# Fewer and larger loads at the start and end of a one-token attention kernel: first K whole, last V in 2 pieces, output projection in 4

## The chip, the cores and the metric

The kernel runs on one core of a Trainium2 chip. The metric is the device time of one execution in microseconds (us). The kernel before took 652.0 us, the median of 3 runs (651.78 to 652.06).

Two numbers are used below. The *time* is the metric. The *span* runs from the first to the last instruction of the trace, and it is listed for every run. The time is 1.3 to 2.0 us longer than the span, and that difference changes from run to run: two runs of the kernel before with a span of 650.3 took 651.69 and 652.32 us.

## The reference

One token attends to a cache of 16384 keys and values with 32 heads of 128, followed by an output projection. A small gated MLP of the same token is mixed in.

```python
# cut: helpers and random inputs
q = (x @ wq).reshape(1, 1, 32, 128).transpose(0, 2, 1, 3)       # x: 1 x 1 x 512, wq: 512 x 4096
scores = einsum('bhqd,bhkd->bhqk', q, k_cache) * 128 ** -0.5    # k_cache: 1 x 32 x 16384 x 128, bf16
p = softmax(scores)
o = einsum('bhqk,bhkd->bhqd', p, v_cache)
a = o.transpose(0, 2, 1, 3).reshape(1, 1, 4096) @ wo            # wo: 4096 x 512
b = ...                                                         # gated MLP of x, width 1792
return g * a + (1 - g) * b                                      # g = sigmoid(sum(x * gate_w))
```

K and V are 134 MB each. Nearly all of the 279.6 MB that the kernel reads is K and V, and each byte is used once.

## The kernel before

The loads go through three large SBUF buffers in a fixed order: K0, K1, V0, K2, V1, K3, V2 and so on, each a pair of heads in 128 partitions of 64 KB (8.39 MB). The last buffer takes the output projection `wo`, 32 rows of 512 per partition. The first K, the last K, the last V and `wo` are cut into pieces, so that work can begin before the whole has landed. Each piece has its own semaphore.

```python
K_CUTS = (0, 128, 256)
V_CUTS = (0, 160, 224, 256)
WO_CUTS = (0, 16, 24, 28, 30, 31, 32)
WIDE = 24
...
    for n, kind, i in loads:                       # issued in order by SyncE
        wait = [user[n - 3]] if n >= 3 else [w_free] if buf[n % 3] is setup else []
        ...
        if n == 0:
            cuts, sems = K_CUTS, ld_kf
        elif i == NP - 1:
            cuts, sems = (K_CUTS, ld_kh) if kind == "k" else (V_CUTS, ld_vp)
        for a, b, done in zip(cuts[:-1], cuts[1:], sems):
            sp.op(lambda e, ...: e.dma_start(out=buf[n % 3][:, a * Dh:b * Dh], in_=src[:, a * Dh:b * Dh]),
                  wait=wait if a == 0 else (), inc=(done, 16))
    for j, (a, b) in enumerate(zip(WO_CUTS[:-1], WO_CUTS[1:])):
        sp.op(lambda e, ...: e.dma_start(out=wo[:, a * D:b * D], in_=wo_src[:, a * D:b * D]), ...)
```

`user[n - 3]` is the last reader of the buffer. V1, for example, goes into K1's buffer, so SyncE issues V1's load when ACT has done the first exponentials of K1. VectorE multiplies a K by the query in four quarters and waits for K data at the first and third. TensorE sums the products; ACT takes the exponentials. A V takes TensorE eight *tiles* of 8 matmuls. TensorE's program is one sequence: the last tiles of the last V, the chain to `o2` (the attention output, transposed for the projection), then the projection.

The projection has two forms. The wide one takes 8 rows in a round of 8 matmuls of 512 columns, spread over four column groups. ACT must then copy the bank, and one more pair of matmuls (`ones` times `d_sb`, the *sum* below) adds the groups up. The narrow one takes a row in two matmuls of 256 columns, straight into the result.

```python
    def pe_wide(e):
        warm(e, 1)                                 # one matmul on zeros
        with e.Fori(0, WIDE // WG) as t:           # rounds of 8 rows
            for j in range(WG): ...                # matmul into d_ps, column group 32 * (j % 4)
            registers_first(nc, n, lambda: take(e, wo_s))   # waits for the piece of wo
            fill(e, 1)                             # one matmul on zeros
    w_ok = act.op(lambda e: e.copy(out=d_sb[:, :], in_=d_ps), wait=[(pe.sem, pe.n)], mark=True)
    ...
    for j, (a, b) in enumerate(zip(WO_CUTS[:-1], WO_CUTS[1:])):
        for k in range(max(a, WIDE), b):           # narrow rows
            y_ok = add(o2[:, k:k + 1], wo[:, k * D:(k + 1) * D], [(ld_o[j], 16)] if k == a else (), k == H - 1)
        if b == 28:
            add(ones_f[:, 0:1], d_sb[:, :], [w_ok])   # the sum
```

The softmax here doesn't subtract the row's maximum and nothing guards it: scores larger than these inputs give would overflow.

Of the kernel before, what the change touches and what calls it, by code (L numbers as in the profile page):

```python
# [15 lines left out]
NP = H // 2  # L16
# [19 lines left out]
NT = NG // TG  # L36
ZB = F // 4
K_CUTS = (0, 128, 256)
V_CUTS = (0, 160, 224, 256)
WO_CUTS = (0, 16, 24, 28, 30, 31, 32)  # L40
WIDE = 24
inv_sqrt_dh = float(Dh) ** -0.5


# [132 lines left out]
def gated_mix_kernel(nc, A_x, A_k_cache, A_v_cache, A_wq, A_wo, B_x, B_w_in, B_w_sp, B_b_sp,  # L177
                     B_w_out, gate_w, out):
    def sb(name, shape, dt):
        return nc.alloc_sbuf_tensor(name, shape, dt)  # L180
# [6 lines left out]
    d_sb = sb("d_sb", [P, 512], FP32)  # L187
# [51 lines left out]
    sem = nc.alloc_semaphore  # L239
# [3 lines left out]
        sem(n) for n in ("ld_x", "ld_g", "ld_q", "ld_w", "ld_u", "st_out"))  # L243
    ld_k = [sem(f"ld_k{b}") for b in range(2)]
    ld_v = [sem(f"ld_v{b}") for b in range(2)]
    ld_kf = [sem(f"ld_kf{b}") for b in range(len(K_CUTS) - 1)]
    ld_kh = [sem(f"ld_kh{b}") for b in range(len(K_CUTS) - 1)]
    ld_vp = [sem(f"ld_vp{b}") for b in range(len(V_CUTS) - 1)]
    ld_o = [sem(f"ld_o{b}") for b in range(len(WO_CUTS) - 1)]
    k_s, v_s, mul_s, red_s, sum_s, exp_s, sl_s, pv_s, drn_s, zer_s, wo_s = (  # L250
        sem(n) for n in ("k_s", "v_s", "mul_s", "red_s", "sum_s", "exp_s", "sl_s", "pv_s", "drn_s",
                         "zer_s", "wo_s"))

    ones_f = nc.const_aps.tensor(1.0, [P, P], FP32)
# [216 lines left out]
    def warm(e, n, again=False):  # L471
        for j in range(n):
            args = (m_ps[0], ident[:, :], zero[:, :])
            flags = dict(start=True, stop=True, skip_group_check=True)
            if j or again:
                matmul_again(nc, e, *args, **flags)
            else:
                e.matmul(args[0], lhsT=args[1], rhs=args[2], **flags)  # L478
# [152 lines left out]
    for n, kind, i in loads:  # L631
        wait = [user[n - 3]] if n >= 3 else [w_free] if buf[n % 3] is setup else []
        src = (k_src if kind == "k" else v_src)[i]
        cuts, sems = (0, KP), [(ld_k if kind == "k" else ld_v)[i % 2]]
        if n == 0:
            cuts, sems = K_CUTS, ld_kf
        elif i == NP - 1:
            cuts, sems = (K_CUTS, ld_kh) if kind == "k" else (V_CUTS, ld_vp)
        for a, b, done in zip(cuts[:-1], cuts[1:], sems):
            sp.op(lambda e, a=a, b=b, n=n, src=src: e.dma_start(  # L640
                out=buf[n % 3][:, a * Dh:b * Dh], in_=src[:, a * Dh:b * Dh]),
                wait=wait if a == 0 else (), inc=(done, 16))
    wo_src = A_wo.rearrange("(p k) n -> p (k n)", k=H)
    for j, (a, b) in enumerate(zip(WO_CUTS[:-1], WO_CUTS[1:])):
        sp.op(lambda e, a=a, b=b: e.dma_start(out=wo[:, a * D:b * D], in_=wo_src[:, a * D:b * D]),  # L645
              wait=[user[wo_at - 3]] if a == 0 else (), inc=(ld_o[j], 16))

    def hand(e, loaded, to, n):
        e.wait_ge(loaded, 16).then_inc(to, n)
        e.nop().then_inc(loaded, -16)  # L650

    def pool_pairs(e):
        for j in range(len(ld_kf)):
            hand(e, ld_kf[j], k_s, 1)
        with e.Fori(0, NP // 2 - 1):
            hand(e, ld_k[1], k_s, 2)
            hand(e, ld_v[0], v_s, NT)
            hand(e, ld_k[0], k_s, 2)
            hand(e, ld_v[1], v_s, NT)
        for j in range(len(ld_kh)):  # L660
            hand(e, ld_kh[j], k_s, 1)
        hand(e, ld_v[0], v_s, NT)
        for j, (a, b) in enumerate(zip(V_CUTS[:-1], V_CUTS[1:])):
            hand(e, ld_vp[j], v_s, (b - a) * NT // KP)

    pool.raw(pool_pairs)


# [17 lines left out]
    def pool_wo(e):  # L686
        e.wait_ge(*d_zero)
        e.wait_ge(*o2_ok)
        for j, (a, b) in enumerate(zip(WO_CUTS[:-1], WO_CUTS[1:])):
            if a < WIDE:  # L690
                hand(e, ld_o[j], wo_s, (min(b, WIDE) - a) // WG)

    pool.raw(pool_wo)

    def pe_wide(e):
        va, pa = (counter(e, n, 0) for n in ("wa", "oa"))
        warm(e, 1)
        with e.Fori(0, WIDE // WG) as t:
            w8 = wo[:, bass.ds(t * (WG * D), WG * D)]
# [12 lines left out]
    pe.raw(pe_wide)  # L712
    pe.n += WIDE // WG
    w_ok = act.op(lambda e: e.copy(out=d_sb[:, :], in_=d_ps), wait=[(pe.sem, pe.n)], mark=True)


    def add(lhsT, rhs, wait, mark=False):
        for s in range(NC):
            ok = pe.op(lambda e, s=s: e.matmul(  # L719
                a_ps[32 * s:32 * s + 1, 0:DQ], lhsT=lhsT, rhs=rhs[:, s * DQ:(s + 1) * DQ],  # L720
                start=False, stop=False, skip_group_check=True), wait=wait if s == 0 else (),
                mark=mark and s == NC - 1, inc=(half, 1) if mark and s == 0 else None)
        return ok

    for j, (a, b) in enumerate(zip(WO_CUTS[:-1], WO_CUTS[1:])):
        for k in range(max(a, WIDE), b):
            y_ok = add(o2[:, k:k + 1], wo[:, k * D:(k + 1) * D],
                       [(ld_o[j], 16)] if k == a else (), k == H - 1)
        if b == 28:
            add(ones_f[:, 0:1], d_sb[:, :], [w_ok])  # L730
    for q in (dve, act):
        mine = range(NC)[:NC // 2] if q is dve else range(NC)[NC // 2:]
        for s in mine:
# [26 lines left out]
def build(inputs):  # L760
    import numpy as _np
    import concourse.bacc as _bacc
    from concourse import mybir as _mybir

    nc = _bacc.Bacc("TRN2", target_bir_lowering=False, num_devices=1, dynamic_dma_scratch_size=4096)
    arrays, args = {}, []
    for name in _INS:
        a = _np.ascontiguousarray(inputs[name])
        if a.dtype.kind in "iu":
            a = a.astype(_np.int64)  # L770
        arrays[f"in_{name}_dram"] = a
        args.append(nc.dram_tensor(f"in_{name}_dram", a.shape, _mybir.dt.from_np(a.dtype), kind="ExternalInput").ap())
    for i, (shape, dtype) in enumerate(_OUTS):
        dt = _mybir.dt.from_np(_np.dtype(dtype))
        args.append(nc.dram_tensor(f"out_{i}_dram", shape, dt, kind="ExternalOutput").ap())
    gated_mix_kernel(nc, *args)
    return nc, arrays
# [9 lines left out]
```

## Time and profile before

| | before |
|---|---|
| time, median of 3 | 652.0 us |
| span of the profiled run | 650.5 us |
| read from HBM | 279.6 MB |
| V1's load issued / K2 landed | 85.3 / 96.4 us |
| last V's pieces landed | 631.1, 636.0, 638.5 us |
| `o2` ready | 642.7 us |
| last row of `wo` landed | 648.53 us |
| result copies start | 648.91 us |

Landing times are those of the load's sixteenth semaphore update in the trace.

The page of the kernel before: span, TensorE's line, and from the 40 slices the granted TensorE clock, the DMA share (tenths) and GB/s, and the summary of the chain that ended last.

```profile
span 650.5 us, 7753 instructions
...
PE 428.0 (66%) x2462; PEld 45.7 (7%) x1320; DVE 336.0 (52%) x159; ACT 45.8 (7%) x112; POOL 2.1 (0%) x10
...
PEclk9978797969779696987969798686988968798999
DMA  9999999999999999999899999999998999999898
GB/s 387 449 429 451 443 395 451 451 387 451 451 439 399 451 451 415 423 451 451 387 451 451 435 403 451 451 391 447 451 451 387 451 451 431 407 419 484 387 433 342
...
DMA 4%; PE 0%; SPq 0%; issue 0%; DVE 0%; ACT 0%; ACTq 0%
...
```

The DMA engines are busy in every slice. The packet records show no gap from 1.3 to 648.0 us. A whole K or V lands 19.35 us after the one before it, which is 433 GB/s. The clock row shows that TensorE, 66% busy, keeps changing between full clock and less.

The chain that ended last, in order of time: start us, us, what.

```profile
...
619.79 27.37 DMA bufs<-in_A_wo_dram
...
647.20 1.36 PE ps_all L719 x18
...
648.57 0.32 PE ps_all L719 x2
...
648.91 0.41 DVE res L734
```

Six loads of `wo` are issued from 618.9, when their buffer comes free, and the rest of the tail hangs on them: 18 matmuls in 1.36 us while the last pieces land, the last two at the last landing, and the copy of the result.

The load of V1 in the timeline (start us, us, engine, line; SPq is SyncE's instruction stream, from which loads are issued):

```profile
...
85.32 0.33 SPq L640 DMA_DIRECT2D bufs<-in_A_v_cache_dram  x1
...
```

Parts of the tail in the timeline (start us, us, engine, line, what; PEld is TensorE's weight load; in brackets the idle time before):

```profile
...
631.27 0.14 PEld L106 LDWEIGHTS ps_all<-bufs,p_t 128*8 x8 [2.13 <-issue]
...
638.64 0.14 PEld L106 LDWEIGHTS ps_all<-bufs,p_t 128*8 x8 [1.45 <-issue]
...
642.47 0.19 DVE L683 CAST o<-ps_all 128x32 bf16<-128x32 f32 x1 [0.35 <-PE ps_all L680]
643.57 0.13 PEld L106 LDWEIGHTS ps_all<-bufs,o 128*1 x8 [1.11 <-issue]
...
```

The last V's first tile starts at 631.27, 0.15 us after the first piece landed. Its eighth starts at 638.64, 0.15 us after the last piece. `o2` is the CAST at 642.47. The first wide round starts at 643.57, when 16 rows of `wo` have landed (643.39), not when `o2` is ready. So the compute waits for the loads at each step.

Four stretches of the tail by engine (busy us, count of instructions, granted clock, DMA share, GB/s); two are shown:

```profile
...
core 0: us, PE busy (x) PEld busy (x) DVE busy (x) ACT busy (x) POOL busy (x), PEclk, DMA share, GB/s
...
641.30:644.70 3.40, 2.10 (x21) 0.70 (x23) 0.60 (x3) 0.00 (x0) 0.00 (x0) 1.00 0.99 417
644.70:648.10 3.40, 2.34 (x32) 0.68 (x24) 0.00 (x0) 0.58 (x1) 0.00 (x0) 1.00 0.95 359
...
```

In this run the clock (PEclk) was full in both.

### The profile page before, as it was taken

Reading aid. Unit: us, or ns where it says so; the run is one execution under the profiler, and the core shown is the slowest. Engines: PE = TensorE matmul, PEld = TensorE weight load, DVE = VectorE, ACT = ScalarE, POOL = GpSimd, SP = SyncE. Lnnn points to the kernel's source line nnn. Section 1 sums busy time; section 2 is a strip of 40 time slices with the busy share of each in tenths; the row PEclk is TensorE's granted clock in tenths of the full one; section 3 lists DMA queues with packets and bytes.
Section 4 is the critical chain, followed back from the end, with each engine's and each line's share of the span. In section 5 each row is a group of like instructions: output and inputs, shape, how many; then the busy total and the mean of one; then the engine's idle time right before and its main releaser. Section 6 shows DMA issues by size and latency. Waiting matters only on the chain. (4 is left out here: it accounts for less than half of the span.)

```text
span 650.5 us, 7753 instructions
## 1 busy us (share of the span) xinstructions
PE 428.0 (66%) x2462; PEld 45.7 (7%) x1320; DVE 336.0 (52%) x159; ACT 45.8 (7%) x112; POOL 2.1 (0%) x10
## 2 busy tenths in 40 slices
PE   0576866847487574757857476585747757478766
PEld 0000010000101000010000101000010100101012
DVE  3587708356281745618265370835629075465600
ACT  2201010000001000010100001000010100001011
POOL 1000000000000000000000000000000000000000
PEclk9978797969779696987969798686988968798999
DMA  9999999999999999999899999999998999999898
GB/s 387 449 429 451 443 395 451 451 387 451 451 439 399 451 451 415 423 451 451 387 451 451 435 403 451 451 391 447 451 451 387 451 451 431 407 419 484 387 433 342
DMA packets 6491, 279.60 MB, mean 430 GB/s; under 512 B 727, under 2 KB 986, under 8 KB 1370
## 3 DMA queue, kind: packets, MB, share of 16 engines
q1 hardware_dynamic: 6482, 279.58, 99.6%
q8 instruction: 1, 0.02, 0.0%
q10 hardware_dynamic: 8, 0.00, 0.0%
HBM read 279.58 MB, written 0.00 MB: 430 GB/s over the span
## 5 line engine op out<-in xcount | busy, mean ns | idle before, releaser
L579 DVE TENSOR_TENSOR bufs<-bufs,qb x64 | 281.4, 4418 | 168.6 <-DVEq L86 168.6
L91 PE MATMUL ps_all<-bufs,ident 128*128 x960 | 265.0, 432 | 0.0
L496 PE MATMUL ps_all<-bufs,ident 128*128 x64 | 28.4, 444 | 150.8 <-PEq L86 150.8
L106 PE MATMUL ps_all<-bufs,p_t 128*8 x1024 | 79.1, 384 | 30.6 <-PEq L86 19.9
L564 DVE TENSOR_REDUCE s_sb<-ps_all 128x64 f32<-128x512 f32 x64 | 44.0, 688 | 97.4 <-DVEq L86 97.4
L91 PE MATMUL ps_all<-zero,ident 128*8 128x512 bf16 (+1 forms) x147 | 56.4, 384 | 0.0
L592 ACT ACTIVATE p_t<-s_sb 64x256 f32 (+1 forms) x32 | 13.3, 414 | 440.2 <-ACTq L86 439.8
L496 PEld LDWEIGHTS ps_all<-bufs,ident 128*128 128x128 bf16 x64 | 6.3, 99 | 368.0 <-issue 368.0
L106 PEld LDWEIGHTS ps_all<-bufs,p_t 128*8 x1024 | 17.8, 82 | 163.7 <-issue 163.3
L531 PE MATMUL ps_all<-pick,d_sb 128*128 128x2 f32 x128 | 16.8, 253 | 14.8 <-PEq L86 14.8
L531 PEld LDWEIGHTS ps_all<-pick,d_sb 128*128 128x128 f32 x128 | 15.5, 191 | 22.9 <-issue 22.9
L601 ACT COPY d_sb<-ps_all 128x512 f32<-128x512 f32 x16 | 9.4, 585 | 104.3 <-ACTq L86 104.3
L606 ACT CAST ps_all<-zero 128x512 f32<-128x512 bf16 x15 | 8.8, 589 | 1.7
L478 PE MATMUL ps_all<-zero,ident 128*128 128x512 bf16 x18 | 7.0, 389 | 0.0
L669 DVE RECIPROCAL rl<-ps_all 128x32 f32<-128x32 f32 x1 | 0.4, 358 | 11.2 <-PE ps_all L552 11.2
L672 DVE TENSOR_TENSOR o_sb<-ps_all,rl 128x32 bf16<-128x32 f32 x1 | 0.2, 193 | 11.5 <-PE ps_all L531 11.5
L382 DVE TENSOR_TENSOR bufs<-ps_all,ident 128x896 f32<-128x896 f32 x2 | 2.1, 1085 | 7.7 <-PE ps_all L91 7.7
L592 ACT ACTIVATION_READ_ACCUMULATOR p_t<-s_sb (+1 forms) x32 | 5.9, 185 | 0.0
L322 PE MATMUL ps_all<-xgw,const-float32-1.0 1*128 1x3 f32 x2 | 0.6, 358 | 8.0 <-DVE xgw L318 8.0
L106 PE MATMUL ps_all<-bufs,u 128*1 x14 | 2.6, 372 | 3.3 <-ACT ps_all L428 2.5
L91 PE MATMUL ps_all<-bufs,xb 128*128 x12 | 4.4, 491 | 0.0
L346 PE MATMUL ps_all<-bufs,xb 128*128 x4 | 2.1, 517 | 3.2 <-DMA bufs<-in_B_w_in_dram 3.2
(76 smaller groups left out, 42.8 us busy)
## 6 DMA issues: line engine op xcount, KB each, us to landing
bufs<-in_A_k_cache_dram SPq DMA_DIRECT2D x4, 4096.0 KB, 33.2
bufs<-in_A_v_cache_dram SPq DMA_DIRECT2D x1, 5120.0 KB, 33.9
bufs<-in_A_wq_dram SPq DMA_DIRECT2D x1, 4096.0 KB, 12.2
bufs<-in_A_v_cache_dram SPq DMA_DIRECT2D x1, 2048.0 KB, 38.4
bufs<-in_A_wo_dram SPq DMA_DIRECT2D x1, 2048.0 KB, 24.4
bufs<-in_B_w_in_dram SPq DMA_DIRECT2D x1, 1792.0 KB, 15.4
bufs<-in_A_v_cache_dram SPq DMA_DIRECT2D x1, 1024.0 KB, 40.4
bufs<-in_A_wo_dram SPq DMA_DIRECT2D x1, 1024.0 KB, 26.6
```

The lines of the kernel that those rows point to most:

```text
L91: ins = eng.matmul(out, lhsT=lhsT, rhs=rhs, **flags).ins
L106: ins = eng.matmul(bank[0:m, 0:n], lhsT=lhsT, rhs=rhs, **flags).ins
L346: if n else matmul_on(nc, e, lambda: e.matmul(args[0], lhsT=args[1], rhs=args[2], **flags), [at, (xa, 0)]))
L382: dve.op(lambda e, h=h, zh=zh: e.tensor_tensor(out=zm[:, 2 * h * ZB:2 * (h + 1) * ZB].rearrange("p (b m k) -> p b m k", b=2, k=FhC), in0=z ...
L478: e.matmul(args[0], lhsT=args[1], rhs=args[2], **flags)
L496: matmul_on(nc, e, lambda: e.matmul(s3, lhsT=ident[:, :], rhs=k3[:, :, 0:W], start=True, **flags), [(kw, 0)])
L531: ins = e.matmul(o2, lhsT=d_sb[:, r * Dh:(r + 1) * Dh], rhs=pick[:, r * 2:(r + 1) * 2], start=False, stop=False, skip_group_check=True)
L564: return e.tensor_reduce(out=s_sb[:, c * QK:(c + 1) * QK], in_=s_ps[c % 2].rearrange("p (j w) -> p j w", w=W), axis=AX.X, op=ALU.add)
L579: e.tensor_tensor(out=k3, in0=k3, in1=qi, op=ALU.mult).then_inc(mul_s, 1)
L592: e.activation(out=p_t[rows, bass.ds(at, NG * 8)].rearrange("p (t c) -> p t c", c=8)[:, :, 4 * s:4 * s + 4], in_=s_sb[rows, :].rearrange(" ...
L601: return e.copy(out=d_sb[:, :], in_=d_ps)
L606: e.copy(out=d_ps, in_=zero[:, :]).then_inc(drn_s, 1)
```

## The change

The intent is fewer and larger loads: the first K whole, the last V in 192 + 64 instead of 160 + 64 + 32, and `wo` in 16, 11, 4 and 1 rows instead of 16, 8, 4, 2, 1 and 1. With 11 rows in one piece, only the first 16 go the wide way. The sum of the wide part is moved in front of all narrow rows.

```diff
-V_CUTS = (0, 160, 224, 256)
-WO_CUTS = (0, 16, 24, 28, 30, 31, 32)
-WIDE = 24
+V_CUTS = (0, 192, 256)
+WO_CUTS = (0, 16, 27, 31, 32)
+WIDE = 16
...
-    ld_kf = [sem(f"ld_kf{b}") for b in range(len(K_CUTS) - 1)]
...
-        if n == 0:
-            cuts, sems = K_CUTS, ld_kf
-        elif i == NP - 1:
+        if i == NP - 1:
             cuts, sems = (K_CUTS, ld_kh) if kind == "k" else (V_CUTS, ld_vp)
...
-        for j in range(len(ld_kf)):
-            hand(e, ld_kf[j], k_s, 1)
+        hand(e, ld_k[0], k_s, 2)
...
+    add(ones_f[:, 0:1], d_sb[:, :], [w_ok])
     for j, (a, b) in enumerate(zip(WO_CUTS[:-1], WO_CUTS[1:])):
         for k in range(max(a, WIDE), b):
             y_ok = add(...)
-        if b == 28:
-            add(ones_f[:, 0:1], d_sb[:, :], [w_ok])
```

## The prediction

> **What bounds the kernel now.** The loads. The page has the DMA share at 9 tenths in nearly every slice, 279.6 MB over a 650.5 us span. From the trace's landing times every 8.39 MB K or V tile lands 19.35 us after the one before (433 GB/s); the Trainium skill, "DMA: Bandwidth & Descriptors", section "Where 436 GB/s comes from", gives 435 GB/s as the ceiling, and this trace agrees. The packet records show no gap from 1.3 us to 648.0 us. The chain of waits is a V-buffer release at 618.9, 27.4 us of output-projection (Wo) loads, then TensorE, the copy and the store. So only a gap in the stream, or the tail after it, can move the time. The last row of Wo lands at 648.53; its two matmuls start at 648.57; the result copies start at 648.91.
>
> **First K whole.** VectorE began on its first half at 31.8; the whole lands at about 38.0, so it begins 6.4 us later. The K0 and K1 stages take about 26.4 us each (timeline), so the load of V1, issued at 85.3 when K1's scores are done, moves to about 91.7. The stream needs it by about 95, since K2 lands at 96.4. No gap, but only some 3 us of slack. Worth nothing (0.07 us of stream).
>
> **Last V in 192 + 64.** In the timeline the last V runs 8 tiles of 0.93 us; seven start from 631.3 (first piece landed 631.1), the eighth from 638.6 (last piece landed 638.5). Now the first piece lands at about 633.5, and all eight run after it: eighth tile at about 640.5. TensorE idles from 629.3 to 633.7; the granted clock was already 0.68 in 630 to 635, and tiles at half clock took 1.28 us. "TensorE: Matmul & The Clock Gate", Part 1, says a window of some 3.4 us must be busy before full clock returns; the trace's clock changes at multiples of 3.41 us. The last V ends 2.0 us later (1.6 to 2.5), and so does o2 (642.7 to 644.7).
>
> **Wo 16, 11, 4, 1.** Stream: 4 fewer small loads; rows of 1 KB took 0.33 to 0.35 us, of 8 KB 0.31, so the last byte lands about 0.15 to 0.2 us earlier, near 648.35. TensorE: one wide round (0.9 us) goes away, 8 rows go narrow at 0.107 us each. The sum of the wide part is now added first, so every narrow matmul waits for it. Wide rounds at 644.9 and 645.8, ACT copy 646.5 to 647.1, the sum 0.43 us, 11 rows 1.18 us, 4 rows 0.43 us: the last row starts at about 649.2, after all of Wo has landed, against 648.57.
>
> **Net.** The tail becomes TensorE-bound: +0.65 us, less 0.05 us. Predicted 652.6 us, range 651.9 to 653.4. Faster by over 2%: 0.005; within 2%: 0.985; slower: 0.01.
>
> **What would show it.** Issues: V1 at about 91.7, no gap in DMA. Last V's tiles without a break from 633.7 to 641. Last Wo landing near 648.35, but no wait of the narrow matmuls for a Wo load: they wait for ACT's copy of the wide sum; the chain runs V load, V tiles, o2, wide, copy, narrow.
>
> **What would make it wrong.** V1 issued after 95: a gap of up to 2 us, paid in full. The clock warm in the last V: +0.3 us only. The clock low in the narrow part: up to +1.5 us. Small loads costing more than read: a gain.

## The result, and the profile after

The changed kernel took 652.31 us in the median of 6 runs (651.73 to 653.12), against 651.94 us for the kernel before in the same rounds (6 runs, 651.66 to 652.14). The ratio was 1.0007 with a 95% interval of 0.9994 to 1.002: the same. Ratios here and below compare runs of the same rounds; they are not quite the ratio of the medians.

The median hides the shape. The six runs fall into two groups, three at 651.73 to 651.92 and three at 652.69 to 653.12, with nothing between. The profiled run is the longest of them. I ran the changed kernel once more (experiment `after_again`). Over all 11 runs, 4 spans are 650.3 to 650.5 and 7 are 651.3 to 652.7. The kernel before, in the 36 runs that were made beside the experiments, has 34 spans at 650.2 to 650.7 and two of 651.3 and 651.4. So the changed kernel is as fast as before in a third of its runs and 1 us or more slower in the others; the mean span is 651.25 against 650.43.

The page of the profiled (long) run:

```profile
span 651.7 us, 7753 instructions
...
PEclk9959788969779796977969698796979968698988
...
GB/s 383 466 414 451 451 418 418 451 451 394 442 451 447 394 447 451 430 406 451 451 422 414 451 451 406 430 451 451 394 442 451 442 394 451 451 404 432 434 422 303
...
PE 1%; ACT 0%; DVE 0%; issue 0%
...
```

The stream is as full as before until the last slice. The chain no longer has a load in it.

The chain that ended last, in order of time:

```profile
...
644.47 0.82 PE ps_all L106 x8
645.29 0.43 PE ps_all L91
645.72 0.87 PE ps_all L106 x8
...
646.61 0.59 ACT d_sb L710
...
647.24 2.81 PE ps_all L715 x36
...
650.08 0.41 DVE res L729
```

Set against the chain of before, the loads are gone: two wide rounds, ACT's copy, then 36 matmuls in 2.81 us without a wait. The last row of `wo` had landed at 648.06, 2.0 us before the result was copied.

V1's load:

```profile
...
91.57 0.33 SPq L637 DMA_DIRECT2D bufs<-in_A_v_cache_dram  x1
...
```

The same parts of the tail:

```profile
...
633.44 0.13 PEld L106 LDWEIGHTS ps_all<-bufs,p_t 128*8 x8 [4.54 <-issue]
...
634.29 0.63 PE L91 MATMUL ps_all<-zero,ident 128*8 128x512 bf16 x1
...
635.57 0.63 PE L91 MATMUL ps_all<-zero,ident 128*8 128x512 bf16 x1
...
638.66 0.38 PE L91 MATMUL ps_all<-zero,ident 128*8 128x512 bf16 x1
...
639.31 0.38 PE L91 MATMUL ps_all<-zero,ident 128*8 128x512 bf16 x1
...
639.85 0.41 PEld L106 LDWEIGHTS ps_all<-bufs,p_t 128*8 x8 [0.24 <-issue]
...
643.94 0.19 DVE L679 CAST o<-ps_all 128x32 bf16<-128x32 f32 x1 [0.35 <-PE ps_all L676]
644.43 0.13 PEld L106 LDWEIGHTS ps_all<-bufs,o 128*1 x8 [0.51 <-issue]
...
```

The first tile of the last V starts at 633.44, the eighth at 639.85, 1.2 us later than before. These are weight loads, which here run ahead of the matmuls: the fill behind the eighth tile is at 640.60 against 639.12, 1.48 us later. The fills (L91) show the clock: 1.28 us apart at 634.29 and 635.57, 0.65 us apart at 638.66 and 639.31. `o2` starts at 643.94 instead of 642.47, and the wide rounds now wait for it, not for their load (643.07).

The last three of the four stretches:

```profile
...
641.30:644.70 3.40, 2.86 (x26) 1.56 (x24) 0.60 (x3) 0.76 (x2) 0.00 (x0) 1.00 0.97 408
644.70:648.10 3.40, 3.15 (x24) 0.53 (x16) 0.00 (x0) 0.59 (x1) 0.00 (x0) 0.50 0.74 290
648.10:650.00 1.90, 1.90 (x34) 1.30 (x30) 0.00 (x0) 0.00 (x0) 0.00 (x0) 0.99 0.00 0
...
```

From 644.7 to 648.1 TensorE had half clock, through nearly all of the two wide rounds and the sum. No idle time of TensorE in the stretch before (641.3 to 644.7) was longer than 0.25 us, and 2.86 of its 3.40 us count as busy. The busy share does not tell what the clock does next: in the kernel before, TensorE was busy for only 2.10 us of the same stretch (2.22 of 3.41 in the stretch from 642.01 to 645.42, which lies two steps of 3.41 us after its last clock change at 635.19), and its clock stayed full. What ran differs: there two wide rounds of 512 columns a matmul, here, besides matmuls on zeros, the end of the last V and the chain to `o2`, and no wide round before 644.47. Whether this is the cause was not tested.

Why the long run is 1.17 us longer at the start of the result copies (650.08 against 648.91) can be added up from these lines. `o2` was ready at 644.13 instead of 642.66. From there, before: 6.25 us, most of it waiting for loads. After: 0.34 to the first wide matmul, 2.14 for two rounds, 0.63 for the copy, 2.81 for the sum and the rows, 0.03: 5.95. At full clock the two rounds took 1.56 us before (643.60 to about 645.16). The sum and rows took 2.32 us in the later run `after_warm`, whose trace has full clock from 632.2 us to the end. So half clock accounts for about (2.14 - 1.56) + (2.81 - 2.32) = 1.07 us. Without it this chain would end at 649.0, 0.1 us later than before: an estimate from those durations, and close to where the short runs lie.

### The profile page after: what moved, and what is told of

Read it like the earlier page. It is cut to its first block, busy times and chain, and to the rows that moved or that the text cites. A ratio compares the mean times of both kernels' runs of the same rounds, so it can differ in the third digit from the quotient of the medians.

```text
span 651.7 us, 7753 instructions
## 1 busy us (share of the span) xinstructions
PE 424.8 (65%) x2470; PEld 47.8 (7%) x1328; DVE 336.0 (52%) x159; ACT 45.8 (7%) x112; POOL 2.1 (0%) x10
## 5 line engine op out<-in xcount | busy, mean ns | idle before, releaser
L91 PE MATMUL ps_all<-bufs,ident 128*128 x960 | 259.5, 424 | 0.0
L495 PE MATMUL ps_all<-bufs,ident 128*128 x64 | 28.9, 451 | 154.9 <-PEq L86 154.9
L91 PE MATMUL ps_all<-zero,ident 128*8 128x512 bf16 (+1 forms) x146 | 56.6, 388 | 0.0
L91 PE MATMUL ps_all<-bufs,xb 128*128 x12 | 4.1, 462 | 0.0
```

The costliest lines, as they stand in the source:

```text
L91: ins = eng.matmul(out, lhsT=lhsT, rhs=rhs, **flags).ins
L495: matmul_on(nc, e, lambda: e.matmul(s3, lhsT=ident[:, :], rhs=k3[:, :, 0:W], start=True, **flags), [(kw, 0)])
```

## The experiments

My theory: the tail after the last V has become TensorE's, and its length depends on where the clock falls to half. The first K costs nothing. The rivals: the later first K costs; the spread is noise of the loads; the new order or the 11 rows cost by themselves. Twelve runs were made, the first of them of the changed kernel again; all gave correct results. They were run in four groups, each group on one chip together with the kernel before; a ratio is always taken within its group.

### The changed kernel again

No edit.

> The changed kernel once more, for a second profile. My theory (the tail after the last V is now TensorE's, and its length depends on where the clock's 3.41 us windows fall): the runs fall into two groups about 1 us apart, near 651.8 and near 653.0, all at the same DMA pace; the profile of a short run shows full clock in the last 4 us, that of a long one half clock in one window of them. Rival (the spread is DMA noise): a continuous spread, and the last load lands at a different time in short and long runs.

Measured: 653.54 us in the median of 5 (651.84 to 654.17), before 651.78; ratio 1.0019 [1.0005, 1.0033]. Spans: 650.4, 651.4, 651.6, 651.8, 652.7. The profiled run was a long one (651.4). Its trace has half clock from 644.35 to 647.76, 36 matmuls in 2.70 us at the end, and no gap in the stream; its last load landed at 647.90. That is 0.16 us earlier than in the other long run, not later. Two groups were found again, but the long one is not tight (one run of 652.7), and no short run was profiled. So the clock's part was to be tested by filling TensorE's idle time, below.

### One part of the change at a time

`only_k` is the kernel before with the first K whole:

```diff
-        if n == 0:
-            cuts, sems = K_CUTS, ld_kf
-        elif i == NP - 1:
+        if i == NP - 1:
```

> The kernel before with only the first K loaded whole. My theory: V1 is issued near 91.6 instead of 85.3, no gap in the stream, time equal to before within 0.1 us (651.9). Rival (the later first K is what costs): 0.3 to 1 us slower than before, with V1's landing later than 115.7.

Measured: 651.78 us, as before in the same rounds; ratio 0.9994 [0.9981, 1.0008]. Spans 650.1 to 650.4 in all five runs. V1 was issued at 91.37 and landed at 115.57, 19.36 us after K2: no loss. So the first K alone costs nothing, as expected.

This run has a second use. Its clock fell to half in the projection, and it still ended on time. Two stretches of its tail, of which the first has half clock:

```profile
...
643.30:646.70 3.40, 3.21 (x26) 0.60 (x24) 0.00 (x0) 0.00 (x0) 0.00 (x0) 0.50 0.99 398
646.70:650.00 3.30, 2.01 (x25) 0.70 (x20) 0.41 (x1) 0.95 (x2) 0.00 (x0) 1.00 0.27 87
...
```

The old tail has room for this. TensorE waits for loads there anyway, so slow rounds eat waiting time.

`only_v` is the kernel before with the last V in two pieces:

```diff
-V_CUTS = (0, 160, 224, 256)
+V_CUTS = (0, 192, 256)
```

> The kernel before with only the last V cut in 192 and 64. My theory: last V's tiles end 1.5 us later, the three wide rounds start at 644.4, 645.4 and 646.3 and the copy ends at 647.6, still before the last row of the output projection lands at 648.5; so equal to before where the clock stays full (652.0), and up to 1 us longer where it falls, so a mean 0 to 0.6 us above before. Rival (V's cut is harmless): within 0.1 us of before in every run.

Measured: median 652.83 us, ratio 1.0003 [0.9989, 1.0016]. Spans 650.2, 650.3, 651.0, 651.2, 651.4. The chain of the profiled run (651.2) at its end:

```profile
...
647.90 0.59 ACT d_sb L714
...
648.54 1.08 PE ps_all L719 x12
...
649.64 0.41 DVE res L734
```

The copy of three wide rounds ended at 648.49 instead of the 647.6 that I had worked out for full clock, because the clock was half from 644.9 to 648.3. The two groups are there with the V cut alone, as expected.

`only_wo` is the kernel before with the projection's part (the last three hunks of the diff, and `WIDE`).

> The kernel before with only the output projection's part (16, 11, 4, 1 rows, 16 of them wide, the wide sum added first). My theory: o2 is as early as before (642.7), the wide sum is done at 645.8, the 11 rows wait for their load at 646.8, and the last row starts right after the last load lands near 648.2: 0.3 us faster than before (651.6). Rival (the new order of the projection costs by itself): 0.3 to 1 us slower than before.

This was a miss. Measured: median 652.4 us, ratio 1.001 [0.9997, 1.0024]; spans 650.4, 650.8, 651.0, 651.2, 651.8. The profiled run is the shortest, with full clock, and it is no faster than before. Its chain:

```profile
...
619.13 27.55 DMA bufs<-in_A_wo_dram
...
646.72 2.05 PE ps_all L719 x32
...
648.79 0.41 DVE res L733
```

The 11 rows wait for their load at 646.7, and the 32 matmuls behind it take 2.05 us. The last load landed at 648.33, only 0.2 us earlier than before, and the result copies start 0.46 us later; before, that was 0.38 us. I had left out that 11 rows (1.2 us) plus 4 rows (0.43 us) take a little longer than the loads behind them. So even this run gains only 0.1 us of the expected 0.3, and the other four are slower than before, as the rival had it. So the V cut alone (mean span 650.8) and the projection alone (651.0) each bring longer runs, against 650.4 for the kernel before and 651.25 for the whole change. What makes them longer is tested next.

### Filling TensorE's idle time

`after_warm` adds matmuls on zeros to the changed kernel: 16 ahead of the last V, one more at each of three places in the chain to the wide rounds, 3 behind them.

```diff
             stop=True).then_inc(sl_s, 1)
+            warm(e, 16)
...
-    pe.raw(lambda e: warm(e, 1))        # twice
+    pe.raw(lambda e: warm(e, 2))
...
-        warm(e, 1)                      # before the wide rounds
+        warm(e, 2)
...
+        warm(e, 3)                      # behind the wide rounds
```

> The changed kernel with matmuls on zeros added where TensorE would idle in the tail: 16 before the last V, one more at each of the three places that already had one, 3 behind the wide rounds. Work is only added. My theory (long runs are half clock in the tail): no clock record of half in the last 20 us, the last V's tiles done at 640.2 instead of 640.6, 36 narrow matmuls in 1.9 to 2.2 us instead of 2.8, and every run has a span of 650.4 to 650.8: the long runs of 651.3 and more are gone. Rival (long runs have another cause, a later load or the store): the same share of long runs, or more, since work was added.

Measured: spans 650.7, 650.7, 650.8, 650.9, 651.3 (times 652.10 to 652.71). The profiled run is the 651.3 one. The end of its chain:

```profile
...
646.92 0.43 PE ps_all L91 x2
647.36 2.32 PE ps_all L717 x36
...
649.70 0.41 DVE res L731
```

Its clock was full from 632.2 to the end, and the 36 matmuls took 2.32 us. The three matmuls behind the rounds ended too late and delayed the sum by about 0.3 us. The other surplus is in the stream: V1's load was issued at 92.41, and V1 landed 19.94 us after K2 instead of 19.35. The stream lost 0.59 us there, and the last load landed at 648.45. The forecast of at most 650.8 in every run was missed by two runs. One of five is above 651, against seven of eleven without the filling: fewer, but the counts are small. The other four are not as short as the unfilled short runs (650.7 to 650.9 against 650.3 to 650.5).

`only_wo_warm` is `only_wo` with such filling (8 ahead of the last V, one more at two places, 4 in front of and 4 behind the wide rounds).

> The kernel before with only the output projection's part (only_wo), and matmuls on zeros in the idle times of the tail: 8 before the last V, one more at each of two places, 4 before and 4 behind the wide rounds. My theory (only_wo was longer than before in four of five runs because 16 narrow rows at half clock take 3.4 us where full clock takes 1.7): full clock through the tail, every run at 650.3 to 650.5, none at 651 or above. Rival (11 rows behind one load are too much by themselves): 650.8 to 651.8 as before the filling.

Measured: spans 650.3, 650.3, 650.3, 650.5, 651.2. Four of five are as expected, against one of five without the filling. The profiled run is again the odd one. Its clock was half from 640.9 to 644.4, before the wide rounds; there the filling itself ran at half speed and delayed them (first round at 644.8), and the filling behind the rounds held the sum back by another 0.5 us (from 646.75 to 647.27). So the 11 rows are not too much by themselves: four runs and the shortest of `only_wo` end on time with them. That the clock makes them so in the longer runs of `only_wo` is likely, but none of those was profiled. Filling that stands in the chain can itself cost.

`before_warm` is the kernel before with the filling, without the part behind the rounds.

> The kernel before with the same filling (none behind the wide rounds). My theory: its usual runs are bound by the last load and stay at 650.2 to 650.5; its rare longer ones (651.3, 651.4) are gone. Rival (rare long runs are the loads' noise): they stay, about one in nine.

Measured: 651.74 us, ratio 1.0 [0.9986, 1.0013]; spans 650.2 to 650.3. The usual run is bound by the loads, as expected. That it had no long run proves little, since the kernel before has two in 36.

`after_warm_k` is `after_warm` with the first K in halves again.

> The changed kernel with the filling (after_warm), but the first K in halves as before. My theory (the one run of 651.3 among the five of after_warm was V1's load, issued at 92.4, too late, which cost 0.59 us of stream; the other runs are the clock-free length of this tail): V1 is issued at 85 to 86, no gap, and all five spans are 650.6 to 650.9. Rival (the run of 651.3 had another cause): about one run in five at 651.3 again.

Measured: spans 650.8, 650.8, 650.8, 650.9, 651.2. V1 was issued at 86.81 and the stream had no gap in the profiled run (650.9). The run of 651.2 was not expected, and it was not profiled. So I can't say that the gap at V1 is the only cause of single longer runs of the filled kernel; what made this one longer stays open.

### The sum behind the 11 rows

`late_sum`:

```diff
-    add(ones_f[:, 0:1], d_sb[:, :], [w_ok])
     for j, (a, b) in enumerate(zip(WO_CUTS[:-1], WO_CUTS[1:])):
         for k in range(max(a, WIDE), b): ...
+        if b == 27:
+            add(ones_f[:, 0:1], d_sb[:, :], [w_ok])
```

> The changed kernel with the wide part's sum added behind the 11 rows instead of first. My theory: in a profile with the clock at half, the 11 narrow rows start at 646.5 (their load) instead of 648.0 and the last row ends 0.6 to 0.8 us earlier: spans of long runs 650.7 to 651.1 instead of 651.3 to 652.7, of short ones 650.2 to 650.4 as before. Rival (the order of the sum is harmless, the rows themselves cost): spans as those of the changed kernel.

Measured: median 652.19 us, ratio 1.0006 [0.9992, 1.0019]; spans 650.6, 650.6, 650.8, 650.8, 651.4. The profiled run (650.8) had half clock from 643.8 to 647.2, about where the changed kernel's long runs have it. Its chain:

```profile
...
645.51 0.85 PE ps_all L106 x8
...
646.75 2.39 PE ps_all L715 x32
...
649.17 0.41 DVE res L730
```

ACT's copy is no longer in the chain. The rows start at 646.75 instead of 648.05, and the result copies 0.91 us earlier than in the first profile of the changed kernel, 0.64 us earlier than in the second (649.81). That is about the gain that was expected, but not all of it is the order's: the half clock ended at 647.2 here and at 648.1 and 647.8 in the other two, so it slowed fewer of the rows. An estimate, taking half of the 0.94 and 0.58 us by which it ended earlier as lost work, leaves 0.4 us for the order. Of the spans, four are under those of the changed kernel's long runs (651.3 and more), but no short run of 650.2 to 650.4 came in these five.

### How much slack the first K has

The first K itself was not delayed: a kernel that did so had a race on a semaphore and was not run. Instead, `only_k` got idle ACT copies ahead of K1's exponentials, which hold back V1's load and nothing else that is near its limit.

```diff
         take(e, red_s)
+        if isinstance(i, int) and i == 1:
+            for j in range(5):          # 10 in v1_late10
+                e.copy(out=idle[:, j * 512:(j + 1) * 512], in_=zero[:, :])
```

> The kernel with the first K whole alone (only_k), with 5 idle ACT copies before K1's exponentials, some 2.5 to 3 us, so that V1's load is issued at about 94. My theory (the first K whole costs nothing because the load it delays still has some 3 us of slack): no gap, V1 lands at 115.6 as before, span 650.4. Rival (each us of delay at the start is paid at the end): span 2.5 to 3 us longer.

> The same with 10 copies, 5 to 6 us, so that V1's load is issued at about 96.5 to 97.2, behind the end of K2's data (about 95.9). My theory: the stream stops for about 1.5 to 2.3 us after K2 and the whole of it is in the time: V1 lands at 117.1 to 117.9, span 651.9 to 652.7. Rival (the stream catches up, or the tail hides it): span unchanged at 650.4.

Both missed, in the same direction. `v1_late5`: V1 issued at 94.41, landed 20.33 us after K2 instead of 19.35, a loss of 0.98 us; spans 651.8, 651.8, 652.2, 652.8; ratio 1.0026. `v1_late10`: issued at 96.49, landed 22.14 us after K2, a loss of 2.79 us; spans 653.3 to 654.6; ratio 1.0053. The stretches around the gap in `v1_late10`:

```profile
...
92.00:94.00 2.00, 1.79 (x26) 0.27 (x16) 0.00 (x0) 2.00 (x5) 0.00 (x0) 1.00 1.21 524
94.00:96.00 2.00, 1.80 (x27) 0.27 (x16) 0.00 (x0) 2.00 (x5) 0.00 (x0) 1.00 0.00 0
96.00:98.00 2.00, 1.80 (x23) 0.27 (x16) 1.55 (x1) 0.97 (x5) 0.00 (x0) 1.00 1.47 492
...
```

No data packet begins between 94 and 96 us. K2 landed at 96.13, but its last packets began by 93.3 and ended by 95.7; the first packets of V1 began at 97.45, 0.96 us after the issue. So the deadline lies well before the landing of the load ahead. Taken together: issued at 91.57 (the changed kernel) no loss, at 92.41 a loss of 0.59, at 94.41 of 0.98, at 96.49 of 2.79. What is lost early is in the time at the end: the five `only_k` spans are 650.1 to 650.4, those of `v1_late10` 3 us or more longer. Part of the surplus in `v1_late5` (0.3 and 0.2 us later in the stream) has no cause that I found. Why 92.41 loses, although its first packets could have begun on time, is open as well; the loss is on one DMA engine of 16, whose first packet of V1 began last, at 95.76, and took 2.98 us instead of 2.42, while the others went on without a gap. It is one profile, but no other profile shows a loss of that size between two whole loads except the two that were delayed on purpose. With the first K whole and no idle copies, the profiles have V1's issue anywhere from 90.83 to 92.41, so a long run of the changed kernel (that of 652.7, say) may hold such a loss too; neither of the two that were profiled does.

### A version from these findings

`best` has the K and V of before, the filling, and `wo` cut so that at full clock each piece (0.107 us a row) is done before the next lands (0.31 us a row):

```diff
-WO_CUTS = (0, 16, 27, 31, 32)
+WO_CUTS = (0, 16, 24, 29, 31, 32)      # the rest as only_wo_warm, 3 behind the rounds
```

> First K in halves and last V in 3 pieces as before, the output projection in 16, 8, 5, 2 and 1 rows, 16 of them wide, the sum first, the filling as above with 3 behind the wide rounds. My theory: at full clock a row costs TensorE 0.107 us and the load 0.31, so each piece is done before the next lands; the last row starts at its landing near 648.3: 650.1 to 650.3 in every run, 0.1 to 0.3 us under before. Rival: no better than before (650.4), because the loads set it.

Measured: spans 650.1, 650.2, 650.2, 650.3, 650.9; median time 651.93 against 651.83, ratio 1.0002 [0.9989, 1.0016]. Four of five spans are 0.1 to 0.3 us under the usual 650.4, but the times show no gain. No version here beats the kernel before.

## Why the prediction was right or wrong

The predicted 652.6 us (651.9 to 653.4) held the measured 652.31. The place and the mechanism were right, as far as the two profiles of the changed kernel show, both of long runs: the tail became TensorE's, narrow rows wait for ACT's copy and not for a load, the chain has no load. Part of the agreement in size is luck, for two terms were mis-sized in opposite directions.

- **The stream** ("the last byte lands about 0.15 to 0.2 us earlier"): nearly right. From the landing of the V ahead to the last row it is 29.30 us after and 29.54 before, 0.24 us less. It is worth nothing, since the tail no longer ends with it.
- **The last V** ("the last V ends 2.0 us later ..., and so does o2"): mis-sized. `o2` came 1.47 us later. The first piece landed at 633.29, not 633.5, and the eighth tile started at 639.85, not 640.5. Half clock lasted from 631.1 to 637.9, but the tiles it slowed were caught up afterwards at 0.65 us a tile, so it cost almost nothing: from the first tile to the eighth it was 6.4 us, where I had allowed 6.8.
- **The projection**: the sequence was right, and so was 0.107 us a row at full clock. The step that failed is the clock. I had put "The clock low in the narrow part: up to +1.5 us" under what would make the prediction wrong. It seems to be the usual case: 7 of 11 runs are long, and half clock is worth about 1.07 us in the profiled one. At full clock the same chain ends only 0.1 us later than before. The single number 652.6 lies in the gap between two groups of runs.
- **The first K** ("No gap, but only some 3 us of slack"): the outcome held in both profiles of the changed kernel and in `only_k` (V1 issued at 91.57, 91.25 and 91.37; predicted 91.7), but the slack was mis-sized. I counted to the landing of K2 less 1 us. The runs show a loss at 92.41 already, so it was under 0.9 us.

The Trainium skill, "TensorE: Matmul & The Clock Gate", Part 1, "What's actually happening", says that the window is free-running and "doesn't reset when your kernel starts". This agrees: the half-clock window is at 644.7 to 648.1 and at 644.4 to 647.8 in the changed kernel's two profiles, and at 643.8 to 647.2 in that of `late_sum`, which does the same work up to there. Each is 3.41 us long. That the short runs are those without half clock in this place is not seen in a profile of a short run of the changed kernel. It is concluded from the filling and from the one full-clock profile of `only_wo`, its shortest run. The counts of the filling are: above 651, 7 of 11 without it and 2 of 10 with it (`after_warm` and `after_warm_k`); above 650.5 in the projection's part alone, 4 of 5 without and 1 of 5 with. They are too few to settle it: a split as uneven comes by chance alone with a probability of 0.08 and 0.21 (Fisher's exact test). What the durations give is the size, 1.07 us in a long run; that the clock alone makes the two groups stays likely and not shown.

## What to carry to other kernels

In this kernel, bound by its loads, the pieces at the end keep the compute behind the last landing short. When they were merged, the saved loads brought 0.24 us, while the compute that had waited for loads moved onto the critical path and brought the variations of its clock with it. Look at the runs one by one: two groups, with a median between them, point at a state that the profile of a single run shows only half. And count the slack of a load from the start of the last packets ahead of it, not from their landing: here those began at 92.6 to 93.3, issues up to 91.57 lost nothing, and those at 92.41, 94.41 and 96.49 did.

## What the Trainium skill lacked or had wrong

- "TensorE: Matmul & The Clock Gate", "Why this matters for your kernels", advises no idle gaps of more than about 3 us between bursts. Here the clock fell to half at 644.7 although no idle time in the 3.4 us before was longer than 0.25 us and the records had TensorE busy for 2.86 of 3.40 us. The page knows such a case ("A second HAM failure mode: psum-queue depth-cycling" tells of short idle times between groups of matmuls that make the clock swing), but it does not say how much work a window must hold. The busy time of the records is not the measure: in the kernel before, 2.22 of 3.41 us kept the clock full.
- The same page, Part 1, says that for modeling the penalty of the warm-up is under 1% of a typical span and that a count of slow matmuls is not to be fitted. It does not speak of half clock that comes back in a short tail. There it is under 1% too (1.07 of 651 us, an estimate), but larger than everything else that the change does, and it probably splits the runs into two groups.
- "DMA: Bandwidth & Descriptors" gives 435 GB/s as the ceiling ("Where 436 GB/s comes from"); 433 was measured over 8.39 MB loads. It agrees. But the same section also says that for transfers between HBM and SBUF the HBM side binds, at about 358 GB/s; for this program, which runs on one core, that did not hold.
- The same page, "Specifications", gives about 0.6 us of first-byte latency for loads from SyncE. Here the first packets began 0.96 us after the start of the issuing instruction (96.49 to 97.45), which itself took 0.33 us: 0.63 us from its end. Counted so it agrees; the page does not say from where it counts.
- The same page does not say how early a load must be issued to keep the stream closed. Here, with 64 KB packets of 2.42 us, a load issued 4.6 us before the landing of the one ahead lost nothing, one issued 3.6 us before it lost 0.59 us, and one 1.7 us before it lost 0.98 us.
